# Two Strassen operands of a squared-ReLU layer: made where they are used, or made early and carried through DRAM

## The chip, the cores and the metric

The kernel runs on one core of a Trainium2 chip. The metric is the device time of one execution in microseconds (us). Runs of one set were taken on one chip, next to runs of the kernel before. Of each kernel one execution was also recorded by the hardware profiler. TensorE does the matmuls here and writes their sums into PSUM tiles; VectorE and ScalarE empty these (a "bank-emptying addition" is a VectorE operation that does so), and GpSimd does some of the elementwise work.

## The reference

```python
# attention: 8 batches, 8 heads, 576 positions, head size 64, all float32
scores = q @ k.T / sqrt(64)
ret = (scores * Dmat) @ v             # Dmat: gamma_h ** (i - j) for i >= j, else 0
x = ret as (4608 tokens, 512)
# feed-forward, d_ff 2048
h = maximum(x @ w_in, 0)
out = (h * h) @ w_out                 # g below is h * h, transposed
```

## The kernel before

The two large products are done by a Strassen-like scheme with seven products in place of eight, twice nested in the second one. A block is 512 tokens, and there are nine.

*First half.* For each block and for each of four slices of d_ff (`mp`), seven products (`j` = 0 to 6) give the four quarters of g. VectorE then makes four more operands from them, and all seven go to DRAM. The attention of later tokens runs between the products.

*Second half.* Each of the seven operands of each of the nine blocks is one round (63 rounds, `k`): it is fetched from DRAM, divided again into four, VectorE makes four inner sums, and TensorE does seven small products of eight matmuls.

```python
PRODUCTS = (("A11", "B11", "a"), ("S2", "T2", "b"), ("S1", "T1", "c"), ("A12", "B21", "a"),
            ("S3", "T3", "b"), ("S4", "B22", "c"), ("A22", "T4", "b"))   # left, right, PSUM bank

    def g_sums(n, mp):                       # first half, after product 6 of a slice
        g = g_of(mp)
        return [                             # one of them behind each of the next products
            lambda: nc.vector.tensor_tensor(g["S1"], g["S3"], g["A22"], op=ALU.add),       # L555
            lambda: nc.vector.tensor_tensor(g["S2"], g["S1"], g["A11"], op=ALU.subtract),  # L556
            lambda: nc.vector.tensor_tensor(g["S3"], g["A11"], g["S3"], op=ALU.subtract),  # L557
            lambda: nc.vector.tensor_tensor(g["S4"], g["A12"], g["S2"], op=ALU.subtract),  # L558
            lambda: nc.sync.dma_start(g_dram[n, :, :, 2 * mp:2 * mp + 2, :]..., g_room[mp % 2]...),
        ]
    # ... cut: in ffn_in, the additions that empty PSUM banks
        elif j == 1: nc.vector.tensor_tensor(u2, p, p1, op=ALU.add)                        # L629
        elif j == 2: nc.vector.tensor_tensor(p15, p, p1, op=ALU.add)                       # L631
        elif j == 4: nc.vector.tensor_tensor(g["A22"], p, p15, op=ALU.add)                 # L636
        elif j == 5: nc.vector.tensor_tensor(g["S3"], p, u2, op=ALU.add)                   # L640
        else:        nc.vector.tensor_tensor(g["A12"], p, p1, op=ALU.add)                  # L643
    # ... cut: the second half's loop
    for k in range(N_K + 1):
        sums_next = inner_sums(k + 1)        # four VectorE operations, L859 to L862
        inner(k, 0)                          # one small product: 8 matmuls, L909
        for e in range(3):
            inner(k - 1, 4 + e)              # product 4 is emptied by L925, needed by product 6
            if e == 2: outer(k - 1)          # up to two additions, L964
            inner(k, 1 + e)
            sums_next[e]()
            f = next(steps_0, None); f and f()   # block 0's own sums, in narrow strips
        sums_next[3]()
        fetch_g(k + 4)
```

The order in which each engine gets its work is the order of this code. Block 0 takes another path: it is multiplied without the seven products, stored, and its sums are made strip by strip during the second half (`sums_0`).

Of the kernel before, what the change touches and what calls it, by code (L numbers as in the profile page):

```python
# [9 lines left out]
F32 = mybir.dt.float32  # L10
# [3 lines left out]
ALU = mybir.AluOpType  # L14
# [4 lines left out]
HT = TOK // 2  # L19
# [7 lines left out]
PRODUCTS = (  # L27
    ("A11", "B11", "a"),
    ("S2", "T2", "b"),
    ("S1", "T1", "c"),  # L30
    ("A12", "B21", "a"),
    ("S3", "T3", "b"),
    ("S4", "B22", "c"),
    ("A22", "T4", "b"),
)
# [5 lines left out]
def kernel(  # L41
# [33 lines left out]
    nc = tc.nc  # L75
# [9 lines left out]
    N_M = N_DF // 2  # L85
    N_MP = N_M // 2
    N_MQ = N_M // 2
    N_BLK = n_tok // TOK
    NP = len(PRODUCTS)
# [5 lines left out]
    dram = ctx.enter_context(tc.tile_pool(name="dram", bufs=1, space=bass.MemoryType.DRAM))  # L95
# [18 lines left out]
    WI_SLOT = {n: j for j, n in enumerate(("A11", "A12", "S3", "A22", "S1", "S2", "S4"))}  # L114
    w_out = [W[(4 + j) % NP].rearrange("p (m s f) -> p m s f", m=N_MQ, s=NP) for j in range(NP)]
    WO_SLOT = {n: j for j, n in enumerate(("B11", "T3", "B21", "B22", "T1", "T2", "T4"))}
    w2_dram = dram.tile([NP, 128, N_MQ, NP * 128], F32, name="w2_dram")
    g_dram = dram.tile([N_BLK, NP, 128, N_M, HT], F32, name="g_dram")

    room = const.tile([128, 15872], F32, name="room")  # L120
    g_room = [room[:, j * 3584:(j + 1) * 3584].rearrange("p (s m t) -> p s m t", s=NP, m=2) for j in range(2)]
    p_room = [room[:, 7168 + j * 1536:7168 + (j + 1) * 1536].rearrange("p (s m t) -> p s m t", s=3, m=2) for j in range(2)]
    xs_room = room[:, 10240:11776].rearrange("p (s c t) -> p s c t", s=3, c=2)
    xT_room = [room[:, 11776 + j * 2048:11776 + (j + 1) * 2048].rearrange("p (c t) -> p c t", c=N_DM) for j in range(2)]
    G_ORDER = tuple(p[0] for p in PRODUCTS)
    QUARTERS = ((0, 1), (3, 5), (6, 7))
    SUMS = ((1, 3), (4, 6))
    assert G_ORDER == ("A11", "S2", "S1", "A12", "S3", "S4", "A22")

    loaded = {}  # L130
    N_EARLY = TOK // C
# [104 lines left out]
    def sum_w_in(mp):  # L236

        a11, a12, a21, a22, s1, s2, s4 = (w_in[mp][:, :, j, :, :].rearrange("p m c f -> p m (c f)") for j in range(NP))
        return [lambda: nc.vector.tensor_tensor(s1, a21, a22, op=ALU.add),
                lambda: nc.vector.tensor_tensor(s2, s1, a11, op=ALU.subtract),  # L240
                lambda: nc.vector.tensor_tensor(s4, a12, s2, op=ALU.subtract),
                lambda: nc.vector.tensor_tensor(a21, a11, a21, op=ALU.subtract)]
# [93 lines left out]
    for half in range(2):  # L336
        at = slice(CH * half, CH * half + CH)
# [191 lines left out]
    def fetch_w2(j):  # L529
        nc.sync.dma_start(w_out[j].rearrange("p m s f -> p m (s f)"), w2_dram[WO_SLOT[PRODUCTS[j][1]], :, :, :])  # L530

# [14 lines left out]
    sums = {}  # L546

    def g_of(mp):
        return {name: g_room[mp % 2][:, s, :, :] for s, name in enumerate(G_ORDER)}

    def g_sums(n, mp):

        g = g_of(mp)
        return [
            lambda: nc.vector.tensor_tensor(g["S1"], g["S3"], g["A22"], op=ALU.add),  # L555
            lambda: nc.vector.tensor_tensor(g["S2"], g["S1"], g["A11"], op=ALU.subtract),  # L556
            lambda: nc.vector.tensor_tensor(g["S3"], g["A11"], g["S3"], op=ALU.subtract),  # L557
            lambda: nc.vector.tensor_tensor(g["S4"], g["A12"], g["S2"], op=ALU.subtract),  # L558
            lambda: nc.sync.dma_start(g_dram[n, :, :, 2 * mp:2 * mp + 2, :].rearrange("s p m t -> p s (m t)"),
                                      g_room[mp % 2].rearrange("p s m t -> p s (m t)")),  # L560
        ]
# [4 lines left out]
    def some(count=1):  # L566
        for f in queue[:count]:
            f and f()
        del queue[:count]

    def first_in(j, halves=(0, 1)):

        assert n_made[0] > j
        wi, m, e = pieces[j]
        mp, mm = divmod(m, 2)
        p = ps_f.tile([128, 2, HT], F32, tag="f", name="h_ps")
        w = w_in[mp][:, mm, 2 * e:2 * e + 2, :, :].rearrange("p s c f -> p (s c) f")
        lo, hi = halves[0], halves[-1] + 1
        p = p[:, lo:hi, :]
        for c in range(N_DM):  # L580
            nc.tensor.matmul(p.rearrange("p h t -> p (h t)"), lhsT=w[:, c, :], rhs=xT[0][:, c, lo * HT:hi * HT],  # L581
                             start=(c == 0), stop=(c == N_DM - 1))

        t = g_room[mp % 2][:, 3:7:3, mm, :] if e else g_room[mp % 2][:, 0:5:4, mm, :]
        t = t[:, lo:hi, :]
        nc.scalar.activation(t, p, AF.Relu)

        some(2)
        queue.append(lambda: nc.vector.tensor_tensor(t, t, t, op=ALU.mult))
        if mm and e and hi == 2:  # L590
            queue.append(lambda: [nc.sync.dma_start(
                g_dram[0, a:b, :, 2 * mp:2 * mp + 2, :].rearrange("s p m t -> p s (m t)"),
                g_room[mp % 2][:, a:b, :, :].rearrange("p s m t -> p s (m t)")) for a, b in QUARTERS])
        if j >= N_W1 - 4:

            sums_w.setdefault(0, sum_w_in(0)).pop(0)()
            if n_next[0] > 1:
                if 1 not in sums_x:
                    sums_x[1] = sum_x(1)
                sums_x[1].pop(0)()  # L600
# [74 lines left out]
    def block_steps(n):  # L675
        if n == 0:
            seconds = [(0, first_in, j, (1,)) for j in range(N_HALF)]
            return seconds + [(0, first_in, j) for j in range(N_HALF, N_W1)]
        return [(n, ffn_in, n, mp, j) for mp in range(N_MP) for j in range(NP)]

    def step():
        n, f, *args = steps.pop(0)
        done[0] += 1
        f(*args)
# [141 lines left out]
    late1 = ctx.enter_context(tc.tile_pool(name="late1", bufs=1))  # L826
# [9 lines left out]
    N_K = N_BLK * NP  # L836
    BLOCKS = list(range(1, N_BLK)) + [0]

    def A(k):
        return A_room[k % len(A_room)].rearrange("p (m t) -> p m t", m=N_M)  # L840

    def fetch_g(k):
        if k < N_K:
            nc.sync.dma_start(A(k), g_dram[BLOCKS[k // NP], k % NP, :, :, :])

    def lefts(k):

# [24 lines left out]
    def sums_0():  # L872

        for m in range(N_M):
            t = late1.tile([128, NP, HT], F32, tag="g0", name="g0")

            def move(parts, out):
                for a, b in parts:
                    there = g_dram[0, a:b, :, m, :].rearrange("s p t -> p s t")
                    nc.sync.dma_start(*((there, t[:, a:b, :]) if out else (t[:, a:b, :], there)))  # L880

            a11, s2, s1, a12, s3, s4, a22 = (t[:, j, :] for j in range(NP))
            yield lambda: move(QUARTERS, False)
            for _ in range(8):
                yield None
            for to, x, y, op in ((s1, s3, a22, ALU.add), (s2, s1, a11, ALU.subtract), (s3, a11, s3, ALU.subtract),
                                 (s4, a12, s2, ALU.subtract)):
                yield lambda to=to, x=x, y=y, op=op: nc.vector.tensor_tensor(to, x, y, op=op)
            yield lambda: move(SUMS, True)
            for _ in range(3):  # L890
                yield None
# [3 lines left out]
    def inner(k, i):  # L895
# [12 lines left out]
        for m in range(N_MQ):  # L908
            nc.tensor.matmul(p, lhsT=s["lefts"][left][:, m, :], rhs=w_out[j][:, m, WO_SLOT[right], :],  # L909
                             start=(i in OPENS and m == 0), stop=(i in CLOSES and m == N_MQ - 1),  # L910
# [60 lines left out]
    n_last = 0  # L971
    while steps:
        n, f, *args = steps[0]
        if n == N_BLK - 1:
            if n_last in (0, 5, 10, 15):
                fetch_g(n_last // 5)
            if n_last in (2, 9, 16, 23):
                fetch_w2(2 + n_last // 7)
            if n_last == N_MP * NP - 5:
                for f in inner_sums(0):  # L980
                    f()
            n_last += 1
        step()
    some(len(queue))
    fetch_w2(NP - 1)
    steps_0 = sums_0()
    for k in range(N_K + 1):
        assert k + 4 < N_K - NP or next(steps_0, None) is None
        sums_next = inner_sums(k + 1)
        if k < N_K:  # L990
            inner(k, 0)
        for e in range(3):
            if k > 0:
                inner(k - 1, 4 + e)
            if e == 2 and k > 0:
                outer(k - 1)
            if k < N_K:
                inner(k, 1 + e)
            if sums_next[e]:
                sums_next[e]()  # L1000
            f = next(steps_0, None)
            f and f()
        if sums_next[3]:
            sums_next[3]()
        fetch_g(k + 4)


# [44 lines left out]
```

## Time and profile before

| | before |
|---|---|
| first set: median (range), runs | 990.98 (989.02 to 992.9), 3 |
| span of the profiled execution | 987.4 us |
| TensorE matmul / weight load / VectorE busy | 98% / 87% / 78% of the span |
| DMA traffic | 219 MB |

The views that matter are shown in the prediction. To read them: L909 is a line of the program; `h_a`, `h_b`, `h_c` are PSUM tiles of the first half and `o_a`, `o_b`, `o_c` those of the second; `x8` counts merged instructions; a bracket at the end of a line is the time for which the engine sat idle before it, and what ended that.

### The profile page before, as it was taken

The numbers are of one execution on the slowest core, as the hardware profiler recorded it, in microseconds if no ns is written. First come the engines' busy times: TensorE is split into PE (matmuls) and PEld (weight loads), VectorE is DVE, ScalarE is ACT, GpSimd is POOL, SyncE is SP. The second block draws the span as 40 slices with busy tenths as digits, with TensorE's granted clock in tenths as the row PEclk, the third lists the DMA queues.
The fourth block names the chain that finished last, engine by engine and source line by source line (L and its number), as shares of the span: only waits on it lengthen the run. The fifth ranks groups of instructions, "written<-read, shape, count | busy, mean of one in ns | idle before, by whom it ended". The sixth has DMA issues, their size and how long they took to land.

```text
span 987.4 us, 24367 instructions
## 1 busy us (share of the span) xinstructions
PE 967.8 (98%) x10404; PEld 863.0 (87%) x10404; DVE 769.7 (78%) x1434; ACT 234.1 (24%) x573; POOL 127.8 (13%) x121
## 2 busy tenths in 40 slices
PE   7899999999999999999999999999999999999998
PEld 6645787888888888888888889999999999999998
DVE  4889898768888988888886677777777777777765
ACT  3454573752223222322211100000000000000000
POOL 3221222312213121222201000000000000000000
PEclk7999999999999999999999999999999999999999
DMA  9985657755687687779449999675584657556351
GB/s 203 244 223 152 175 158 214 194 144 182 216 278 241 186 277 229 222 234 264 143 179 333 403 383 346 227 280 163 223 282 145 258 206 274 192 203 217 125 214 44
DMA packets 185037, 219.22 MB, mean 222 GB/s; under 512 B 118624, under 2 KB 135008, under 8 KB 175968
## 3 DMA queue, kind: packets, MB, share of 16 engines
q1 hardware_dynamic: 182816, 217.13, 67.3%
q8 instruction: 82, 1.34, 0.6%
q10 hardware_dynamic: 2112, 0.52, 0.3%
q14 instruction: 27, 0.22, 0.1%
HBM read 128.23 MB, written 89.39 MB: 220 GB/s over the span
## 4 chain that ended last, share of the span: by engine, by line
PE 88%; DVE 9%; issue 1%; DMA 1%; ACT 1%; SPq 0%; DVEq 0%; ACTq 0%
PE o_b L909 17%; PE h_b L617 15%; PE o_c L909 11%; PE o_a L909 11%; PE h_a L617 10%; PE h_c L617 10%; PE h_ps L581 4%; PE x_ps L458 3%; PE sc_ps L436 2%; PE x_ps L493 2%; PE t_ps L415 2%; DVE room L624 1%; DVE w L229 1%; PE u_ps L461 1%; DMA w<-in_moe_w_in_dram 1%
## 5 line engine op out<-in xcount | busy, mean ns | idle before, releaser
L617 PE MATMUL h_b<-room,w 128*128 128x256 f32 x736 | 177.4, 384 | 3.6 <-DVE room L636 2.6
L617 PEld LDWEIGHTS h_b<-room,w 128*128 128x128 f32 x736 | 137.3, 190 | 24.4 <-DVE room L636 3.8
L909 PE MATMUL o_b<-w,room 128*128 128x128 f32 x1168 | 144.5, 276 | 0.2 <-DVE room L860 0.2
L909 PEld LDWEIGHTS o_b<-w,room 128*128 128x128 f32 x1168 | 137.3, 192 | 0.5 <-DVE room L860 0.4
L909 PE MATMUL o_c<-w,room 128*128 128x128 f32 x1008 | 123.0, 275 | 0.0
L909 PEld LDWEIGHTS o_c<-w,room 128*128 128x128 f32 x1008 | 117.7, 192 | 0.0
L617 PE MATMUL h_c<-room,w 128*128 128x256 f32 x480 | 114.4, 382 | 0.7 <-DVE room L631 0.7
L617 PE MATMUL h_a<-room,w 128*128 128x256 f32 x448 | 107.5, 383 | 0.0
L617 PEld LDWEIGHTS h_c<-room,w 128*128 128x128 f32 x480 | 90.6, 190 | 13.3 <-DVE room L631 1.1
L617 PEld LDWEIGHTS h_a<-room,w 128*128 128x128 f32 x448 | 84.0, 190 | 11.6
L909 PE MATMUL o_a<-w,a 128*128 128x128 f32 x688 | 85.6, 275 | 0.0
L634 POOL TENSOR_TENSOR room<-room 128x512 f32<-128x512 f32 x32 | 35.7, 1116 | 364.4 <-ACT room L633 304.4
L909 PEld LDWEIGHTS o_a<-w,a 128*128 128x128 f32 x688 | 81.3, 192 | 0.1
L923 ACT COPY r<-o_a 128x128 f32<-128x128 f32 x53 | 14.1, 265 | 271.7 <-PE o_a L909 235.8
L624 DVE SCALAR_TENSOR_TENSOR room<-room 128x512 f32<-128x512 f32 x96 | 70.3, 733 | 3.3
L581 PE MATMUL h_ps<-room,w 128*128 128x512 f32 (+1 forms) x152 | 59.6, 540 | 1.1 <-ACT room L515 0.7
L376 POOL TENSOR_TENSOR q_ld<-q_ld,dv 128x512 f32<-128x512 f32 (+1 forms) x39 | 46.9, 1202 | 81.6 <-DMA q_ld<-in_q_dram 78.1
L636 DVE TENSOR_TENSOR room<-h_b,room 128x512 f32<-128x512 f32 x32 | 22.1, 689 | 41.9 <-PE h_b L617 40.1
L458 PEld LDWEIGHTS x_ps<-qk,v_ld 64*64 64x64 f32 x1152 | 40.2, 137 | 14.4 <-issue 11.5
L458 PE MATMUL x_ps<-qk,v_ld 64*64 64x64 f32 x1152 | 49.6, 226 | 1.9 <-ACT u_sb L496 1.9
L581 PEld LDWEIGHTS h_ps<-room,w 128*128 128x128 f32 x152 | 28.2, 194 | 24.0 <-issue 20.5
L404 ACT COPY qk<-flip 32x256 f32<-32x256 f32 x120 | 48.3, 402 | 1.7
(111 smaller groups left out, 1440.5 us busy)
## 6 DMA issues: line engine op xcount, KB each, us to landing
g_dram<-room SPq DMA_DIRECT2D x32, 1792.0 KB, 7.4
a<-g_dram SPq DMA_DIRECT2D x43, 1024.0 KB, 7.1
room<-g_dram SPq DMA_DIRECT2D x20, 1024.0 KB, 6.5
w<-w_dram SPq DMA_DIRECT2D x7, 1792.0 KB, 12.3
out_dram<-room SPq DMA_DIRECT2D x17, 512.0 KB, 3.3
w<-in_moe_w_in_dram SPq DMA_DIRECT2D x16, 512.0 KB, 6.0
w<-in_moe_w_out_dram SPq DMA_DIRECT2D x16, 512.0 KB, 4.2
v_ld<-in_v_dram SPq DMA_DIRECT2D x31, 256.0 KB, 3.6
```

Of the source, the lines that this page charges most:

```text
L376: engine.tensor_tensor(t, t, dv[:cs, :, NCH + ci:NCH + ci + 1].to_broadcast([cs, H, D]), op=ALU.mult)
L404: nc.scalar.copy(*moves.pop(0)[1:])
L415: nc.tensor.transpose(p[:, h, j, hp, :], loaded[i][j][rows(h), 2 * hp:2 * hp + 2, :], ident[rows(h), rows(h)])
L436: nc.tensor.matmul(sc[e][rows(h), hp, :], lhsT=kT[rows(e), hp, t], rhs=qT[rows(e), hp, t], start=True, stop=True, skip_group_check=True)
L458: own.append(lambda hp=hp, e=e, b=b: nc.tensor.matmul(x_at(hp, b, h), lhsT=s["vs"][rows(h), 2 * hp + b, :], rhs=s["ret"][rows(h), e, hp, : ...
L493: nc.tensor.matmul(x_at(hp, b, h), lhsT=u[rows(e), hp, :], rhs=s["qT"][rows(e), hp, CH * h:CH * h + CH], start=clears(b, hp // 2), stop=Fa ...
L581: nc.tensor.matmul(p.rearrange("p h t -> p (h t)"), lhsT=w[:, c, :], rhs=xT[0][:, c, lo * HT:hi * HT], start=(c == 0), stop=(c == N_DM - 1))
L617: nc.tensor.matmul(p[:, mm, :], lhsT=w[:, c, :], rhs=xs[n][right][:, c, :], start=(j in OPENS and mm == 0 and c == 0), stop=(j in CLOSES a ...
L624: nc.vector.scalar_tensor_tensor(t, t, 0.0, t, op0=ALU.max, op1=ALU.mult)
L634: nc.gpsimd.tensor_tensor(g["A11"], g["A11"], g["A11"], op=ALU.mult)
L636: nc.vector.tensor_tensor(g["A22"], p, p15, op=ALU.add)
L909: nc.tensor.matmul(p, lhsT=s["lefts"][left][:, m, :], rhs=w_out[j][:, m, WO_SLOT[right], :], start=(i in OPENS and m == 0), stop=(i in CLO ...
```

## The change

The intent: S2 = S1 − A11 and S4 = A12 − S2 can be made from operands that are on chip in the second half anyway. So they need not be made in the first half, nor written, nor read. Two of VectorE's four sums per slice go from the first half, whose VectorE is the busier one (84% against 74%), to the second; five operands instead of seven go through DRAM. Since S1 must be there before S2 is made, it is fetched one round earlier.

```diff
--- before.py
+++ after.py
@@ -114,18 +114,17 @@
     WI_SLOT = {n: j for j, n in enumerate(("A11", "A12", "S3", "A22", "S1", "S2", "S4"))}
     w_out = [W[(4 + j) % NP].rearrange("p (m s f) -> p m s f", m=N_MQ, s=NP) for j in range(NP)]
     WO_SLOT = {n: j for j, n in enumerate(("B11", "T3", "B21", "B22", "T1", "T2", "T4"))}
+    G_KEPT = ("A11", "S1", "A12", "S3", "A22")
     w2_dram = dram.tile([NP, 128, N_MQ, NP * 128], F32, name="w2_dram")
-    g_dram = dram.tile([N_BLK, NP, 128, N_M, HT], F32, name="g_dram")
+    g_dram = dram.tile([N_BLK, len(G_KEPT), 128, N_M, HT], F32, name="g_dram")
 
     room = const.tile([128, 15872], F32, name="room")
-    g_room = [room[:, j * 3584:(j + 1) * 3584].rearrange("p (s m t) -> p s m t", s=NP, m=2) for j in range(2)]
+    g_room = [room[:, j * 2560:(j + 1) * 2560].rearrange("p (s m t) -> p s m t", s=5, m=2) for j in range(2)]
     p_room = [room[:, 7168 + j * 1536:7168 + (j + 1) * 1536].rearrange("p (s m t) -> p s m t", s=3, m=2) for j in range(2)]
     xs_room = room[:, 10240:11776].rearrange("p (s c t) -> p s c t", s=3, c=2)
     xT_room = [room[:, 11776 + j * 2048:11776 + (j + 1) * 2048].rearrange("p (c t) -> p c t", c=N_DM) for j in range(2)]
-    G_ORDER = tuple(p[0] for p in PRODUCTS)
-    QUARTERS = ((0, 1), (3, 5), (6, 7))
-    SUMS = ((1, 3), (4, 6))
-    assert G_ORDER == ("A11", "S2", "S1", "A12", "S3", "S4", "A22")
+    QUARTERS = ((0, 1), (2, 5))
+    SUMS = ((1, 2), (3, 4))
 
     loaded = {}
     N_EARLY = TOK // C
@@ -546,16 +545,14 @@
     sums = {}
 
     def g_of(mp):
-        return {name: g_room[mp % 2][:, s, :, :] for s, name in enumerate(G_ORDER)}
+        return {name: g_room[mp % 2][:, s, :, :] for s, name in enumerate(G_KEPT)}
 
     def g_sums(n, mp):
 
         g = g_of(mp)
         return [
             lambda: nc.vector.tensor_tensor(g["S1"], g["S3"], g["A22"], op=ALU.add),
-            lambda: nc.vector.tensor_tensor(g["S2"], g["S1"], g["A11"], op=ALU.subtract),
             lambda: nc.vector.tensor_tensor(g["S3"], g["A11"], g["S3"], op=ALU.subtract),
-            lambda: nc.vector.tensor_tensor(g["S4"], g["A12"], g["S2"], op=ALU.subtract),
             lambda: nc.sync.dma_start(g_dram[n, :, :, 2 * mp:2 * mp + 2, :].rearrange("s p m t -> p s (m t)"),
                                       g_room[mp % 2].rearrange("p s m t -> p s (m t)")),
         ]
@@ -581,7 +578,7 @@
             nc.tensor.matmul(p.rearrange("p h t -> p (h t)"), lhsT=w[:, c, :], rhs=xT[0][:, c, lo * HT:hi * HT],
                              start=(c == 0), stop=(c == N_DM - 1))
 
-        t = g_room[mp % 2][:, 3:7:3, mm, :] if e else g_room[mp % 2][:, 0:5:4, mm, :]
+        t = g_room[mp % 2][:, 2:5:2, mm, :] if e else g_room[mp % 2][:, 0:4:3, mm, :]
         t = t[:, lo:hi, :]
         nc.scalar.activation(t, p, AF.Relu)
 
@@ -840,8 +837,19 @@
         return A_room[k % len(A_room)].rearrange("p (m t) -> p m t", m=N_M)
 
     def fetch_g(k):
-        if k < N_K:
-            nc.sync.dma_start(A(k), g_dram[BLOCKS[k // NP], k % NP, :, :, :])
+
+        j = k % NP
+        if k < N_K and j not in (2, 5):
+            k += j == 1
+            nc.sync.dma_start(A(k), g_dram[BLOCKS[k // NP], G_KEPT.index(PRODUCTS[k % NP][0]), :, :, :])
+
+    def made(k):
+
+        if k >= N_K or k % NP not in (1, 5):
+            return []
+        x, y = (k + 1, k - 1) if k % NP == 1 else (k - 2, k - 4)
+        at = [slice(2 * e, 2 * e + 2) for e in range(4)]
+        return [lambda at=at: nc.vector.tensor_tensor(A(k)[:, at, :], A(x)[:, at, :], A(y)[:, at, :], op=ALU.subtract) for at in at]
 
     def lefts(k):
 
@@ -872,19 +880,18 @@
     def sums_0():
 
         for m in range(N_M):
-            t = late1.tile([128, NP, HT], F32, tag="g0", name="g0")
+            t = late1.tile([128, len(G_KEPT), HT], F32, tag="g0", name="g0")
 
             def move(parts, out):
                 for a, b in parts:
                     there = g_dram[0, a:b, :, m, :].rearrange("s p t -> p s t")
                     nc.sync.dma_start(*((there, t[:, a:b, :]) if out else (t[:, a:b, :], there)))
 
-            a11, s2, s1, a12, s3, s4, a22 = (t[:, j, :] for j in range(NP))
+            a11, s1, a12, s3, a22 = (t[:, j, :] for j in range(len(G_KEPT)))
             yield lambda: move(QUARTERS, False)
-            for _ in range(8):
+            for _ in range(6):
                 yield None
-            for to, x, y, op in ((s1, s3, a22, ALU.add), (s2, s1, a11, ALU.subtract), (s3, a11, s3, ALU.subtract),
-                                 (s4, a12, s2, ALU.subtract)):
+            for to, x, y, op in ((s1, s3, a22, ALU.add), (s3, a11, s3, ALU.subtract)):
                 yield lambda to=to, x=x, y=y, op=op: nc.vector.tensor_tensor(to, x, y, op=op)
             yield lambda: move(SUMS, True)
             for _ in range(3):
@@ -979,12 +986,15 @@
             if n_last == N_MP * NP - 5:
                 for f in inner_sums(0):
                     f()
+            if n_last >= N_MP * NP - 4:
+                made(1)[n_last - N_MP * NP]()
             n_last += 1
         step()
     some(len(queue))
     fetch_w2(NP - 1)
     steps_0 = sums_0()
     for k in range(N_K + 1):
+        sums_g = [None] * (k % NP == NP - 1) + made(k + 2)
         assert k + 4 < N_K - NP or next(steps_0, None) is None
         sums_next = inner_sums(k + 1)
         if k < N_K:
@@ -998,10 +1008,15 @@
                 inner(k, 1 + e)
             if sums_next[e]:
                 sums_next[e]()
-            f = next(steps_0, None)
+            if sums_g:
+                f = sums_g.pop(0)
+            else:
+                f = next(steps_0, None)
             f and f()
         if sums_next[3]:
             sums_next[3]()
+        for f in sums_g:
+            f()
         fetch_g(k + 4)
 
 
```

## The prediction

> **What bounds the kernel now.** I first read the page's busy times, then the stretch table for three stages: attention interleaved with the first half of the feed-forward (to 545 us), the last first-half block (to 589), and the second half.
>
> ```profile
> core 0: us, PE busy (x) PEld busy (x) DVE busy (x) ACT busy (x) POOL busy (x), PEclk, DMA share, GB/s
> 108.00:545.00 437.00, 430.45 (x5174) 365.87 (x5173) 365.59 (x588) 149.34 (x343) 95.62 (x84) 1.00 0.70 218
> 545.00:589.00 44.00, 44.00 (x206) 38.82 (x205) 31.72 (x48) 4.14 (x7) 4.15 (x4) 1.00 0.99 396
> 589.00:981.00 392.00, 391.76 (x3504) 391.40 (x3503) 289.44 (x664) 33.16 (x125) 0.00 (x0) 1.00 0.60 215
> ```
>
> The columns are busy us with instruction counts, then granted clock, DMA share and GB/s. TensorE has no room in the last stage: 391.76 of 392 us. In the first it is idle 437 − 430.45 = 6.55 us. VectorE is busy 84% of the first stage and 74% of the last, so it has room in both. DMA is nearly full only from 545 to 589, and TensorE loses nothing there (44.00 of 44).
>
> Next I read TensorE's waits in the first stage (two windows, 110 to 300 and 300 to 545): line, what it waited for, total us, times, longest.
>
> ```profile
> PE h_b L617 <- DVE room L636: 2.0, 2, 1.7
> PE h_b L617 <- DVE room L542: 1.0, 1, 1.0
> PE h_c L617 <- DVE room L631: 0.7, 1, 0.7
> ...
> PE x_ps L458 <- ACT u_sb L496: 1.4, 2, 1.0
> PE sc_ps L436 <- DVE qk L419: 0.7, 1, 0.7
> PE h_b L617 <- DVE room L636: 0.6, 1, 0.6
> ```
>
> They sum to 6.4 us, 5.0 of it behind VectorE. This is the whole prize of the first stage: whatever VectorE is spared, TensorE cannot gain more. The timeline of VectorE around the worst one shows the mechanism:
>
> ```profile
> 147.49 1.50 POOL L376 TENSOR_TENSOR q_ld<-q_ld,dv 128x512 f32<-128x512 f32 x1
> ...
> 148.60 0.94 DVE L558 TENSOR_TENSOR room<-room 128x512 f32<-128x512 f32 x1
> 149.47 1.54 DVE L240 TENSOR_TENSOR w<-w 128x512 f32<-128x512 f32 x1
> 151.04 0.69 DVE L241 TENSOR_TENSOR w<-w 128x512 f32<-128x512 f32 x1
> 151.65 0.68 DVE L636 TENSOR_TENSOR room<-h_b,room 128x512 f32<-128x512 f32 x1
> ...
> 152.38 0.92 PE L617 MATMUL h_b<-room,w 128*128 128x256 f32 x3 [1.66 <-DVE room L636]
> ```
>
> L636, which empties the PSUM bank TensorE needs next, stands behind L558 (S4 of g), a removed operation.
>
> Last, VectorE's timeline of one second-half round, for how far it may run behind:
>
> ```profile
> 701.81 0.29 DVE L925 TENSOR_TENSOR r<-o_b,small 128x128 f32<-128x128 f32 x1 [0.46 <-PE o_b L909]
> 702.78 0.29 DVE L919 TENSOR_TENSOR small<-o_b,small 128x128 f32<-128x128 f32 x1 [0.67 <-PE o_b L909]
> ...
> 704.49 0.29 DVE L921 TENSOR_TENSOR small<-o_c,small 128x128 f32<-128x128 f32 x1 [0.60 <-PE o_c L909]
> ...
> 706.32 0.68 DVE L861 TENSOR_TENSOR room<-a 128x512 f32<-128x512 f32 x1
> 706.92 0.68 DVE L862 TENSOR_TENSOR room<-a,room 128x512 f32<-128x512 f32 x1
> 708.07 0.29 DVE L925 TENSOR_TENSOR r<-o_b,small 128x128 f32<-128x128 f32 x1 [0.46 <-PE o_b L909]
> ```
>
> L925 recurs after 6.26 us: one round, seven groups of eight matmuls, 0.893 us a group. Operations listed at 0.68 us start 0.60 us apart, so 0.605 us is the price of one 128x512 addition in a full queue. VectorE's spare time per round is the sum of the brackets: 0.46 + 0.67 + 0.60 = 1.73 us.
>
> **What the Trainium skill says.** "Perfetto Trace Analysis", section "Identifying the Most-Contended Engine", calls matmul busy share a poor measure and recommends the weight-load share. Here that is 391.40/392 in the second half and 365.87/437 = 84% in the first; the 98% of the first stage hides short gaps, but the trace names no releaser for most of them. "TensorE: Matmul & The Clock Gate", section "Architectural detail", says VectorE's queue is strict FIFO; the wait of L636 behind L240 and L241 agrees, and it means that each added quarter delays every bank-emptying addition behind it. "SBUF — State Buffer", section "SBUF: two separate sides", says a VectorE operation with two SBUF inputs and a GpSimd operation exclude one another for a whole instruction; L240's 1.54 us beside GpSimd against 0.68 agrees. In the second half GpSimd runs nothing, so the moved operations cost 0.605 us there and sometimes twice that where they are removed.
>
> **The change part by part.**
> *Removed, first half:* L556 and L558, 32 each at 708 and 709 ns in the group view; in a full queue about 64 x 0.605 = 38.7 us of VectorE. Little of it lies on the path. I went through the stalls one by one. At 147 and 150 us (0.65 + 1.66) L557 and L558 stood in front; S3 now comes one product earlier, so some 1.5 us disappear from the queue and I count 1.7 with the slowdown beside GpSimd. At 134 us (0.31 shown, some 0.45 in start times) L558 was in front: −0.4. At 430 us (0.59 shown, some 0.75) all three of L556 to L558: −0.7. At 489 us TensorE waited 0.98 for ScalarE's L496, which stood behind a conversion waiting for VectorE's L211, behind L556 and L557: −1.0. At 292 us (0.95) and 322 us (0.73) none of the removed ones is close ahead: −0.4 for both. Sum: −4.2 us.
>
> *Removed, traffic:* two of seven operands are neither written nor read: 2 x 9 blocks x 2 directions x 1.05 MB = 38 MB of 219. No TensorE wait for DMA is listed in these stretches: 0 us.
>
> *Added, second half:* per block of seven rounds, two operands of four quarters: 8 x 0.605 = 4.84 us, 11% of the 43.8 us of a block. They sit in two rounds only. In the round that makes S4, one quarter fits into the 0.60 gap; three follow: 3 x 0.605 − 0.46 = 1.35 us late at the next L925. In the round that makes S2 the first slot is empty, so all four come after the second inner sum: 4 x 0.605 − 0.46 = 1.96 us late. Deadline: TensorE's seventh product adds into the bank that L925 reads. It starts 5 groups (4.47 us) into the round; L925 normally ends 2.27 us into it. So 2.2 us of lateness are free. Both rounds pass, the second with 0.2 us left; the next round's 1.73 us bring VectorE back. I put +0.5 us for nine blocks, for an occasional miss. The first block's strip sums lose two of four operations, but they filled gaps: 0.
>
> *Moved, transition:* four quarters of the first S2 are placed between the last four products of the first half. VectorE was only just in time there: L643 starts at 589.35 after a 0.22 us wait, and the first-half bank it empties is the one that the second matmul group of the second half takes, at 590.04. Four quarters put 4 x 0.605 = 2.4 us ahead of it, minus L558 (1.35 us there, beside GpSimd) and the 0.22: L643 ends about 0.9 us or, with a GpSimd collision, 1.5 us late. TensorE waits +1.2 us. The wait for L860 at 595 us (some 0.4) is then covered, since S2 and S4 no longer stand in front: −0.4. Sum +0.8.
>
> *Total:* −4.2 + 0.5 + 0.8 = −2.9 us: 991.0 − 2.9, rounded to 988.
>
> **The rivals.**
> (a) *VectorE becomes the bound of the second half.* If all added work were exposed, 9 x 4.84 = 44 us: 1035. Against it: after the change VectorE is busy some (289 + 9 x 8 x 0.684)/392 = 86%. A milder form is likelier: each S2 round misses its deadline by 0.5 us, 9 x 0.5 = 4.5 us, giving 992. The 0.2 us margin is its argument.
> (b) *VectorE is the hidden pacer of the first half.* Then much of 38.7 us comes back: 955 to 970. For it: 84% busy and many short gaps. Against: only 6.4 us of named waits, and the stages without waits on VectorE run at the same matmul spacing.
> (c) *DMA was binding from 545 to 589.* At 0.99 share, 17% less traffic looks like several us. But TensorE was busy 44.00 of 44: no change from it.
> (d) *Everything first-half is recovered and the rest is free:* 991 − 6.4 = 984.6.
>
> **Range and chances.** The ends follow from (d), lower by some 2 us for unnamed gaps, and from the mild (a) with no first-half relief: 982.5 to 992.5. The before runs alone spread from 989.0 to 992.9. A gain over 2% (20 us) needs (b): 0.03. A loss over 2% needs (a) in earnest: 0.02.
>
> **What would show each step.** Right: second-half TensorE busy still within 1 us of the stretch; VectorE 86% there; waits on VectorE lines in the first half 2 to 3 us instead of 5.0; a new wait of about 1 us on L643's counterpart at the transition; bytes down from 219 to about 181 MB. Wrong: in the second half, waits of matmuls of product seven on the addition of product five that recur in each block (mild a); a first stage shorter by more than 7 us (b); a stretch before the transition that shortens without fewer VectorE waits (c).

## The result, and the profile after

| | before | changed |
|---|---|---|
| median of the runs (range) | 990.86 (989.02 to 992.9), 4 | 985.65 (985.29 to 986.0), 4 |
| span of the profiled execution | 987.4 | 983.9 |
| VectorE busy, share of the span | 78% | 77% |
| traffic | 219.22 MB | 181.46 MB |

The ratio is 0.9947, 95% interval 0.9927 to 0.9967. (Ratios are the mean time of one kernel's fast runs over that of the other's of the same rounds, so not quite the ratio of the medians quoted.) It is a real gain, of half a per cent, and by a 2% measure "same".

The lines have moved: of the bank-emptying additions L629, L631, L636, L640, L643 are now L626, L628, L633, L637, L640 (so L640 is now the one of product 6, before it was that of product 5); L909 is L916, L925 is L932, L859 to L862 are L867 to L870; the weight sums L239 to L242 are L238 to L241. L852 is new: it makes a quarter of S2 or S4.

The same three stretches, with the columns as in the prediction:

```profile
108.00:545.00 437.00, 434.11 (x5196) 369.48 (x5195) 332.80 (x536) 149.75 (x344) 92.94 (x85) 1.00 0.61 190
545.00:589.00 44.00, 44.00 (x222) 39.09 (x220) 30.91 (x46) 3.81 (x7) 4.13 (x4) 1.00 0.82 307
589.00:981.00 392.00, 391.23 (x3497) 390.46 (x3495) 317.28 (x714) 32.88 (x124) 0.00 (x0) 1.00 0.45 161
```

VectorE lost 365.59 − 332.80 = 32.8 us in the first stretch, and TensorE is busy 3.7 us more of it (the stretches are fixed in time, so this one holds a little more of the changed kernel's work). In the last one VectorE went from 289 to 317 us, 81%, and TensorE lost 0.5 us.

TensorE's waits from 110 to 545 us:

```profile
PE h_b L614 <- DVE room L541: 1.0, 1, 1.0
PE x_ps L457 <- ACT u_sb L495: 0.8, 2, 0.4
PE sc_ps L435 <- DVE qk L418: 0.7, 1, 0.7
PE h_b L614 <- DVE room L633: 0.2, 1, 0.2
```

Of 6.4 us, 2.7 are left, 1.9 of them behind VectorE (5.0 before; the prediction said 2 to 3). The list is short of the true loss: at 134 us it has 0.31 us before the change, while TensorE's start times below lose 0.63 there. The listed waits fell by 3.7 us, the start times gained 4.6. The waits for L631 and most of those for L636 are gone, and ScalarE's L496 (now L495) costs 0.8 instead of 1.4.

The place of the worst stall, at 150 us. In the kernel before, these two stood, among others, ahead of the lines that the prediction shows:

```profile
145.96 0.67 DVE L557 TENSOR_TENSOR room<-room 128x512 f32<-128x512 f32 x1
146.55 1.52 DVE L239 TENSOR_TENSOR w<-w 128x512 f32<-128x512 f32 x1
```

In the changed kernel, GpSimd first, then VectorE and TensorE:

```profile
148.73 1.50 POOL L445 TENSOR_TENSOR v_ld<-v_ld,dv 128x512 f32<-128x512 f32 x1
...
145.60 0.67 DVE L238 TENSOR_TENSOR w<-w 128x512 f32<-128x512 f32 x1
...
146.79 1.06 DVE L239 TENSOR_TENSOR w<-w 128x512 f32<-128x512 f32 x1
147.89 1.43 DVE L240 TENSOR_TENSOR w<-w 128x512 f32<-128x512 f32 x1
149.24 0.68 DVE L633 TENSOR_TENSOR room<-h_b,room 128x512 f32<-128x512 f32 x1
...
149.97 1.99 PE L614 MATMUL h_b<-room,w 128*128 128x256 f32 x8 [0.19 <-DVE room L633]
```

S3's and S4's additions (L557, L558) no longer stand between the weight sums. The weight sums L238, L239 and L240 here are L239, L240 and L241 of the kernel before. L633 starts at 149.24 instead of 151.65, and TensorE waits 0.19 us instead of 1.66.

A round of the second half in which S2 is made, VectorE's timeline first, then TensorE's:

```profile
670.05 0.68 DVE L868 TENSOR_TENSOR room<-room,a 128x512 f32<-128x512 f32 x1
670.65 0.69 DVE L852 TENSOR_TENSOR a<-room,a 128x512 f32<-128x512 f32 x1
...
672.78 0.69 DVE L852 TENSOR_TENSOR a<-room,a 128x512 f32<-128x512 f32 x1
673.38 0.69 DVE L870 TENSOR_TENSOR room<-a,room 128x512 f32<-128x512 f32 x1
673.99 1.29 DVE L852 TENSOR_TENSOR a<-room,a 128x512 f32<-128x512 f32 x2
675.19 0.29 DVE L932 TENSOR_TENSOR r<-o_b,small 128x128 f32<-128x128 f32 x1
...
675.90 1.06 PE L916 MATMUL o_b<-w,a 128*128 128x128 f32 x8
```

The four quarters stand one behind the second inner sum, one behind the third and two behind the fourth. L932 has no bracket any more: VectorE came to it late. It ends at 675.48, and the product that needs it starts at 675.90, without a bracket: 0.42 us were to spare.

*Where the time went.* TensorE executes the same 10,404 matmuls in both programs, so its instructions can be paired by number, and the difference of their start times shows where one trace falls behind the other. In the next table the first trace of the changed kernel is the zero, and differences are counted from its time 120 us, so that the start-up of the kernel is left out. A column says how many us a trace is behind when the changed kernel's is at that time.

| trace, us behind at | 140 | 148.5 | 152 | 300 | 440 | 500 | 586 | 600 | 620 | 980 |
|---|---|---|---|---|---|---|---|---|---|---|
| before | 0.63 | 1.67 | 3.14 | 3.13 | 3.98 | 4.57 | 4.56 | 4.69 | 4.11 | 4.11 |
| before, second trace | 0.64 | 1.68 | 3.14 | 3.13 | 4.01 | 4.60 | 4.59 | 4.72 | 3.96 | 3.96 |
| changed, second trace | 0.00 | 0.00 | 0.00 | -0.02 | -0.01 | 0.00 | 0.00 | 0.00 | 0.24 | 0.24 |
| changed, third trace | 0.00 | 0.00 | 0.00 | -0.02 | -0.01 | -0.01 | -0.02 | -0.03 | -0.07 | -0.06 |

The gain is five steps in the first half, 4.57 us together: 0.63 at 134 us, 1.04 at 148, 1.47 at 150, 0.85 at 430 and 0.59 at 489. Between them the programs run at the same pace to 0.02 us. The transition to the second half gains another 0.13, and the first block of the second half gives 0.58 back. From 620 us on, eight blocks with the added work cost nothing.

*The start-up* is what scatters. The 1,390th TensorE instruction starts at 100.5 us in both traces of before, and at 101.2, 102.9 and 100.2 us in the three of the changed kernel. So one pair of traces alone, 987.4 against 983.9, understates the gain by 0.7 us; the medians of three sets show 4.7 to 5.2 us (990.86 to 985.65, 990.47 to 985.78, 990.18 to 985.43), of which the traces name 4.1. Where the other 0.6 to 1.1 us come from is not shown: the traced start-ups of the changed kernel are not the earlier ones on the whole.

### The profile page after: what moved, and what is told of

The parts are those of the page before. It is cut to its first block, busy times and chain, and to the rows that moved or that the text cites. A ratio compares the mean times of both kernels' runs of the same rounds, so it can differ in the third digit from the quotient of the medians.

```text
span 983.9 us, 24277 instructions
## 1 busy us (share of the span) xinstructions
PE 968.0 (98%) x10404; PEld 863.3 (88%) x10404; DVE 759.3 (77%) x1426; ACT 233.9 (24%) x573; POOL 124.8 (13%) x121
## 2 busy tenths in 40 slices
DMA packets 172012, 181.46 MB, mean 184 GB/s; under 512 B 118144, under 2 KB 132480, under 8 KB 165248
## 4 chain that ended last, share of the span: by engine, by line
PE 87%; DVE 8%; DMA 2%; ACT 1%; issue 1%; SPq 0%; DVEq 0%; ACTq 0%
PE o_b L916 16%; PE h_b L614 15%; PE o_a L916 11%; PE o_c L916 11%; PE h_a L614 10%; PE h_c L614 10%; PE h_ps L578 4%; PE x_ps L457 3%; PE x_ps L492 2%; PE sc_ps L435 2%; PE t_ps L414 2%; DMA g<-g_dram 1%; DVE room L621 1%; DVE w L222 1%; DVE w L225 1%
## 5 line engine op out<-in xcount | busy, mean ns | idle before, releaser
L916 PE MATMUL o_b<-w,room 128*128 128x128 f32 x1168 | 144.4, 275 | 0.2 <-DVE room L868 0.2
L916 PEld LDWEIGHTS o_b<-w,room 128*128 128x128 f32 x1168 | 137.2, 192 | 0.4 <-DVE room L868 0.4
L916 PE MATMUL o_c<-w,room 128*128 128x128 f32 x1008 | 123.0, 275 | 0.0
L916 PEld LDWEIGHTS o_c<-w,room 128*128 128x128 f32 x1008 | 117.7, 192 | 0.0
L916 PE MATMUL o_a<-w,a 128*128 128x128 f32 x688 | 85.6, 275 | 0.0
L916 PEld LDWEIGHTS o_a<-w,a 128*128 128x128 f32 x688 | 81.2, 192 | 0.1
L631 POOL TENSOR_TENSOR room<-room 128x512 f32<-128x512 f32 x32 | 34.0, 1062 | 366.4 <-ACT room L630 295.6
L633 DVE TENSOR_TENSOR room<-h_b,room 128x512 f32<-128x512 f32 x32 | 22.1, 690 | 51.0 <-PE h_b L614 47.5
## 6 DMA issues: line engine op xcount, KB each, us to landing
w<-w_dram SPq DMA_DIRECT2D x7, 1792.0 KB, 10.8
```

What stands on the lines that cost most here:

```text
L631: nc.gpsimd.tensor_tensor(g["A11"], g["A11"], g["A11"], op=ALU.mult)
L916: nc.tensor.matmul(p, lhsT=s["lefts"][left][:, m, :], rhs=w_out[j][:, m, WO_SLOT[right], :], start=(i in OPENS and m == 0), stop=(i in CLO ...
```

## The experiments

The theory, Q: what TensorE gained is the shorter queue of VectorE in front of the bank-emptying additions, stall by stall; the traffic gave nothing; the second half stays free of cost because each added operation ends before a deadline that can be worked out. The main rival, D: the gain is the 38 MB of traffic. Twelve runs were made, of eight new kernels and of the two given ones; all gave correct results, and four sets were timed or looked at together. The table behind each is the same as above.

**The kernel before, again.** No edit.

> The kernel before, run again for the spread of its own stalls. Theory Q (the gain is the queue of VectorE in front of the bank-emptying additions): the same five stalls of TensorE in the first half as in its first profile (near 134, 148, 150, 430 and 489 us, some 4.5 us in start times together), ratio to itself 1.000, runs within 989 to 993. Rival D (the gain is the 38 MB of traffic): says nothing of this run. If the stalls differ by over 1 us from the first profile, the spread of its times (989.0 to 992.9) is in them.

Measured: 989.62 us median (989.06 to 990.55), ratio 1.0003 (0.9987 to 1.0020). Its row is the second of the table above: the same five stalls to within 0.04 us. The spread of the kernel's times is not in them.

**S2 and S4 put back into VectorE's queue, traffic as changed.**

```diff
+    idle_room = [room[:, 6144 + j * 512:6656 + j * 512].rearrange(...) for j in range(2)]   # read by nobody
             lambda: ... g["S1"], g["S3"], g["A22"], op=ALU.add),
+            lambda: nc.vector.tensor_tensor(idle_room[0], g["S1"], g["A11"], op=ALU.subtract),
             lambda: ... g["S3"], g["A11"], g["S3"], op=ALU.subtract),
+            lambda: nc.vector.tensor_tensor(idle_room[1], g["A12"], idle_room[0], op=ALU.subtract),
```

> The changed kernel, with the two removed additions put back into VectorE's queue of the first half at their old places, writing into a spare room that nobody reads; the traffic stays at five operands. Theory Q: the first-half stalls come back, +4 to +5 us, about 990. Rival D: no change, 985.7 within 1.

| us behind the changed kernel at | 140 | 148.5 | 152 | 300 | 440 | 500 | 586 | 600 | 620 | 980 |
|---|---|---|---|---|---|---|---|---|---|---|
| S2 and S4 back in the queue | 0.65 | 1.69 | 3.16 | 3.14 | 4.01 | 4.60 | 5.61 | 6.82 | 6.06 | 6.06 |

Measured: 991.21 us (990.89 to 992.02), ratio to before 1.0017 (1.0003 to 1.0032). TensorE's waits from 110 to 545 us are again those of the kernel before, line by line:

```profile
PE h_b L617 <- DVE room L636: 2.6, 3, 1.7
PE x_ps L458 <- ACT u_sb L496: 1.4, 2, 1.0
...
PE h_c L617 <- DVE room L631: 0.7, 1, 0.7
```

All five steps came back at their places with their sizes, with the smaller traffic. D is refuted as the cause of the first half's gain. The run also shows a cost that was not expected: 2.2 us at the transition, where the put-back sums and the four quarters of the first S2 meet. The change pays nothing there only because it takes S2 and S4 away at the same place.

**S4 alone put back, S2's place left empty.**

```diff
             lambda: ... g["S1"], g["S3"], g["A22"], op=ALU.add),
+            None,
             lambda: ... g["S3"], g["A11"], g["S3"], op=ALU.subtract),
+            lambda: nc.vector.tensor_tensor(idle_room[1], g["A12"], g["A11"], op=ALU.subtract),
```

> As the last, but only S4's addition is put back, at its old place, S2's place is left empty. Theory Q, stall by stall: S4's addition stood in front at 134 (+0.5), 148 to 150 (+0.9 to +1.5) and 430 (+0 to +0.7), not at 489 (0): +1.5 to +2.7 us in all, about 987.7, and no stall over 0.7 us at the 489 us place. Rival D: 985.7 within 1. A third reading, that any addition costs its 0.6 us wherever it stands, would give 32 x 0.6 = 19 us, about 1005.

| us behind the changed kernel at | 140 | 148.5 | 152 | 300 | 440 | 500 | 586 | 600 | 620 | 980 |
|---|---|---|---|---|---|---|---|---|---|---|
| S4 back in the queue | 0.00 | 0.00 | 1.48 | 1.46 | 1.48 | 1.49 | 2.50 | 3.11 | 2.65 | 2.65 |

Measured: 987.28 us (987.10 to 987.84), ratio 0.9977. The sum was met, in part by luck: the first half gave 1.49, the lowest that was expected, and the rest came from a place that was not named. At 150 us it cost 1.48, and at 489 nothing, as expected; but at 134 and 430 us it cost nothing either, and 1.6 us came at the transition. So stalls do not add up operation by operation: one operation ahead was absorbed at 134 and 430, two were not. The third reading, 0.6 us for each of the 32 additions wherever they stand, would have given 1005 and is far off.

**The traffic put back, VectorE's work as changed.**

```diff
# ... cut: g_dram has room for seven operands again
-            lambda: nc.sync.dma_start(g_dram[n, :, ...], g_room[mp % 2]...),
+            lambda: [nc.sync.dma_start(g_dram[n, a:a + b, ...], g_room[mp % 2][:, 0:b]...) for a, b in ((0, 5), (5, 2))],
...
+        if k < N_K and j in (0, 5) and BLOCKS[k // NP]:
+            nc.sync.dma_start(A(k + (j == 0)), g_dram[BLOCKS[k // NP], 5 + (j == 5), :, :, :])
```

> The changed kernel with the traffic put back: in the eight blocks of the first half two more operands are written, copies of A11 and S1, and in the second half they are fetched into the tiles of S2 and S4 before those are made; VectorE's work stays as changed. 33.6 MB more, about 215 MB. Theory Q: 985.7 within 1. Rival D: +4 to +5 us, about 990.

| us behind the changed kernel at | 140 | 148.5 | 152 | 300 | 440 | 500 | 586 | 600 | 620 | 980 |
|---|---|---|---|---|---|---|---|---|---|---|
| traffic back, 215 MB | 0.00 | 0.00 | 0.00 | -0.02 | -0.01 | 0.00 | -0.01 | -0.01 | 3.59 | 3.59 |

Measured: 988.33 us (986.83 to 988.74), ratio 0.9984 (0.9970 to 0.9999): outside what Q expected, and near D's size, yet at another place than D's. In the whole first half the traffic makes no difference of more than 0.02 us. All of the loss is one event at 606 us. VectorE's waits from 590 to 630 us in this run:

```profile
DVE g L897 <- DMA g<-g_dram: 4.7, 1, 4.7
...
DVE room L854 <- DMA room<-g_dram: 1.2, 1, 1.2
```

and in the changed kernel:

```profile
DVE g L895 <- DMA g<-g_dram: 2.4, 1, 2.4
```

The first strip of block 0 lands late, VectorE stands still for it with everything behind it in its queue, and TensorE then waits 2.6 us for an addition. In the changed kernel VectorE's wait for the same strip is half as long. The second wait, 1.2 us, is an artefact of this experiment: it is for a fetch into the tile of S4, which the changed kernel does not have. So the traffic is no source of the first half's gain; at the one crowded place it can cost. How much of the 3.6 us is the delayed strip alone was not separated.

**The changed kernel, again**, as yardstick of the next three.

> The changed kernel again, as the yardstick of this set: 985.3 to 986.0, the same stalls of TensorE as in its first profile (0.57 us near 149, 1.18 near 289, 0.61 near 486, 0.50 near 591, 0.49 near 606 and 0.29 near 613, in start times), ratio 0.993 to 0.997.

Measured: 985.78 us (984.75 to 987.47), ratio 0.9945 (0.9921 to 0.9968). The four times lie wider apart than the 985.3 to 986.0 that was expected. Its trace is a row of the first table: equal to the first trace within 0.02 us from 120 to 600 us.

**Two more quarters in each S2 round.**

```diff
         sums_g = [None] * (k % NP == NP - 1) + made(k + 2)
+        if k % NP == NP - 1:
+            sums_g += made(k + 2)[2:]
```

> The changed kernel with the last two quarters of S2 made twice, at the end of the same round (same values). The changed kernel leaves L932's addition 1.81 us late after an S2 round, with 0.42 us of slack before TensorE's seventh product. Theory Q with the deadline of the prediction: lateness 1.81 + 2 x 0.605 = 3.02, so the product waits 3.02 - 2.23 = 0.79 us in each of the eight S2 rounds inside the second half, and nowhere else: +6.3 us, about 992. Rival H (in the second half VectorE's order does not matter below full occupancy; 16 additions raise it from 81% to 83%): no change, 985.7. Rival S (each addition simply adds its 0.6 us): +9.7 us, about 995.

Measured: 992.59 us (992.20 to 994.27), 6.8 us over the changed kernel of this set. From 620 to 980 us its trace falls 7.51 us behind (from −0.24 to 7.27), in eight equal steps of 0.94, one per S2 round. TensorE's waits from 600 us on:

```profile
PE o_b L916 <- DVE r L932: 5.4, 8, 0.7
```

Eight waits (5.4 us as listed, 7.5 in start times) at the place and on the addition that the deadline names. The size expected was 0.79 each, so the model is 0.15 us short; rival H (free, 985.7) and rival S (9.7 us) are out. This is the limit of the change: VectorE is far from full, 81% before the extra operations, and two operations of 0.6 us at the wrong place of one round in seven cost more than the change has won.

**Strips of block 0 later.**

```diff
-            for _ in range(6):
+            for _ in range(6 + 3 * (m == 0)):
                 yield None
```

> The changed kernel with three more empty steps between the load of the first strip of block 0 and its first addition. Theory L (the 2.39 us in which VectorE waited for that strip made the two stalls near 606 and 613): both go, -0.8 us, about 984.9, and VectorE's wait for g's DMA is under 0.3 us. Rival M (the added quarters of the first block make them, by being packed closer than in later blocks): both stay, 985.7.

Measured: 985.05 us (984.68 to 985.18), ratio 0.9940. In the trace both stalls, near 606 and 613 us, are gone: −0.77 us at 620, and VectorE no longer waits for the strip. Theory L holds, M falls: the quarters of the first block are not at fault. The change itself had brought the strip's first addition forward: its diff cuts the empty steps between a strip's load and this addition from eight to six. VectorE was ready for it 10.8 us after the load was issued (590.42 to 601.19), in the kernel before 17.7 us after (594.46 to 612.17, 2.5 of them a wait for another load). By the times alone (0.7 us in medians) one would not say so; the trace decides.

**Four more operations ahead of the sixth product's addition, and ahead of the seventh's**.

```diff
             if n_last >= N_MP * NP - 4:
                 made(1)[n_last - N_MP * NP]()
+            if n_last == N_MP * NP - 2:        # second kernel: - 1
+                for f in made(1):
+                    f()
```

> The changed kernel with the four quarters of the first S2 made a second time (same values), just ahead of the addition that empties the bank of the sixth product (L637) of the last first-half step: that addition ends 4 x 0.605 = 2.4 us later. Theory B6 (the second matmul group of the second half takes the bank of the sixth product): the group, which in the changed kernel started at once, now waits about 1.6 us (586.2 to 587.8). Theory B7 (as the prediction took it, the bank of the seventh product): the changed kernel's trace already speaks against it, since the group started before L640; here it would wait until L640 has ended, some 3.5 us. In both the span grows by about 2.4 us in all, the rest of it at the first S2 of the inner sums (591 us).

> As the last, but the second making stands behind the sixth product's addition (L637) and ahead of the seventh's (L640). Theory B6: the second group starts without a wait, the whole 2.4 us are seen at the first S2 of the inner sums (591 us). Theory B7: the second group waits about 3.5 us.

First the changed kernel's own lines at the transition, TensorE's and then VectorE's:

```profile
586.21 1.06 PE L916 MATMUL o_b<-w,room 128*128 128x128 f32 x8
...
584.67 0.68 DVE L637 TENSOR_TENSOR room<-h_c,room 128x512 f32<-128x512 f32 x1
...
586.59 0.69 DVE L640 TENSOR_TENSOR room<-h_b,room 128x512 f32<-128x512 f32 x1
```

The second group of the second half starts at 586.21, before the seventh product's bank has been touched (L640, 586.59), so it cannot be waiting for that. With the operations ahead of the sixth, TensorE's waits from 545 us on begin with:

```profile
PE o_b L916 <- DVE room L637: 1.4, 1, 1.4
```

The group now waits, for the sixth product's addition. With the operations behind that addition it does not wait at all; the loss, 2.4 us in both, then comes 3.6 us later, behind L926 and not at the inner sum as expected. Theory B6 holds: the bank that the group takes is the sixth product's. The single times, 987.71 and 988.60 us, agree roughly with the 2.6 and 2.8 us by which the traces end behind; the changed kernel was not run in that set.

**VectorE's order at three places**, an attempt to beat both kernels.

```diff
-        if mp == N_MP - 1 and j in (3, 4, 5) and n_next[0] > n + 1:       # a sum of x for the next block,
+        if mp == N_MP - 1 and j in (3, 4, 5, 6) and n_next[0] > n + 1:    # ahead of S1 of g
...
-    some(len(queue))                 # the last S3 of g and its store
-    fetch_w2(NP - 1)                 # the last weights
...
             f and f()
+            if k == 0 and e == 1:    # now behind the second inner sum of the first round
+                some(len(queue))
+                fetch_w2(NP - 1)
```

> An attempt to beat both kernels by VectorE's order alone: the last S3 of g, its store and the last weight load go behind the second inner sum of the first round of the second half (so the strip load goes ahead of two large transfers), and the second sum of x for the next block goes ahead of S1 of g. Theory Q: the stalls near 289 (-1.0), 591 (-0.5) and 606 to 613 (-0.8) go: -2.3 us, about 983.4. If only the transfers were moved by it and the queue does not matter: -0.8, about 984.9.

Measured: 984.50 us, but with four times between 982.55 and 988.38, ratio 0.9940 (0.9910 to 0.9970) against the changed kernel's 0.9945: inconclusive. So it was run again with more rounds, beside the changed kernel.

> The reordered kernel again, since its four times lay between 982.6 and 988.4 although its trace lost the stalls it was meant to lose. Theory Q with start-up noise: its trace from 50 us on is 2.2 to 2.5 us shorter than the changed kernel's of the same set, whatever the times; the median of six times is 1 to 3 us lower than the changed kernel's. If the order cost something that the one profile did not show: stalls of over 0.5 us at new places after 50 us.

> The changed kernel as the yardstick of this pair: 985 to 987, the stalls after 50 us as in its two earlier traces (near 149, 289, 486, 591, 606 and 613 us); differences between its own runs lie in the first 50 us.

Measured: 982.45 us (981.80 to 983.87, 6 runs), against 985.43 (984.47 to 989.45, 6 runs) of the changed kernel and 990.18 (988.98 to 993.57, 11 runs) of before. Ratios to before: 0.9922 (0.9908 to 0.9935) and 0.9960 (0.9941 to 0.9979), which do not overlap. The changed kernel's trace in this set is the last row of the first table: equal to its first within 0.07 us.

| us behind the changed kernel at | 152 | 300 | 440 | 500 | 586 | 600 | 620 | 980 |
|---|---|---|---|---|---|---|---|---|
| reordered, first trace | -0.41 | -1.43 | -1.42 | -1.41 | -1.41 | -1.90 | -2.66 | -2.66 |
| reordered, repeat | 0.00 | -1.00 | -0.99 | -0.99 | -0.99 | -1.48 | -2.24 | -2.24 |

The three steps are 1.0 at 289, 0.5 at 591 and 0.8 at 606 to 613 us, as expected. The first trace had won 0.46 more near 148 us, which the repeat does not show. Which of the three moves gave the steps at 591 and at 606 to 613 us was not separated (the strips placed later had given the last one alone). What TensorE waits for in the repeat, from 110 us to the end, is

```profile
PE x_ps L457 <- ACT u_sb L495: 0.8, 2, 0.4
PE sc_ps L435 <- DVE qk L418: 0.7, 1, 0.7
PE h_b L614 <- DVE room L633: 0.2, 1, 0.2
```

This version beats both kernels: by the medians it is 7.7 us under the kernel before, by the traces from 120 us on about 6.3 us. In the five traces named above the first 100 us differ by up to 2.7 us, and no experiment here touched those.

## Why the prediction was right or wrong

The range (982.5 to 992.5) held the 985.65, and "within 2%" was right. The direction and the mechanism were right, the size was too small: −2.9 us forecast, −4.1 in the traces from 120 us on, −5.2 in the medians of the first set. By its steps:

| step | forecast | traces |
|---|---|---|
| stall at 134 us | −0.4 | −0.63 |
| stalls at 147 and 150 us | −1.7 | −2.51 |
| stall at 430 us | −0.7 | −0.85 |
| stall at 489 us | −1.0 | −0.59 |
| stalls at 292 and 322 us | −0.4 | 0.0 |
| traffic | 0 | 0 in the first half (tested); not separated at 606 us |
| second half | +0.5 | +0.58, in its first block alone |
| transition | +0.8 | −0.13 |

**First half: right, the largest term mis-sized.** The prediction named the five places, and the experiment with the sums put back returned each. For the pair at 147 and 150 us it counted 1.5 us of removed queue time and 0.2 for the slowdown beside GpSimd; the pair gave 1.04 + 1.47 = 2.51. Redone from the two traces: from the first operation behind L629 to the start of L636 VectorE took 5.69 us before (145.96 to 151.65), and takes 3.64 now (145.60 to 149.24, L238 to L633), 2.05 less. L557 and L558 made up 0.59 + 0.87 = 1.46 of that, from start to start, as counted. The other 0.59 is the slowdown, counted as 0.2: the three weight sums beside GpSimd's operations took 1.52 + 1.54 + 0.69 = 3.75 us before and take 0.67 + 1.06 + 1.43 = 3.16 now. The last 0.46 was left out: against TensorE's matmuls, L629 itself had already started 0.46 us later before the change, in a queue of VectorE that shows no idle time since the stall at 134 us. At 489 us the prediction took both L556 and L557 as gone from the front; but S3 moved into S2's place, so that one addition of 0.60 us went, and 0.59 was won. At 292 and 322 us nothing removed stood close ahead and nothing was won, as argued; the 0.4 put down for chance was wrong. That the sum of the first half came so near (−4.2 against −4.58) is in part luck: one term was short by 0.8 and two were over by 0.4 each. The reordering experiment shows that the first of these is a queue stall all the same: it went when another operation was moved.

**Transition: wrong, and this is the step that failed.** It read: "the first-half bank it empties is the one that the second matmul group of the second half takes, at 590.04". That rested on a coincidence of times, L643's end and the group's start, and on a guess about which of three banks is handed out next. The group takes the bank of the sixth product. That addition ended at 585.35 (584.67 + 0.68), 0.86 us before the group's turn, so no stall arose. The stretch is not free in general: with S2 and S4 put back TensorE lost 2.2 us in it, at other waits, and four more operations lost it 2.4. The second part of the term, −0.4 for the wait on L860, was not won either: the last S1 and S3 and the quarters fill the queue as S1 to S4 had done before, and the wait near 591 us is still there (0.50 us from one matmul's start to the next, 0.51 before, of which the inner sum's L868 is the named cause). It went only by reordering. Replacing +0.8 by −0.1 brings the sum to −3.8.

**Second half: the deadline was right, the reason for the cost wrong, its size right by luck.** Forecast was that L925's addition would be late by 1.35 us in S4 rounds and 1.96 in S2 rounds, with 2.2 allowed. In the trace (start of the addition against the end of the product that it empties) it is 1.21 and 1.81 late, round after round, with 1.02 and 0.42 us left before TensorE's product 6. The deadline itself was tested by the two extra quarters. The +0.5 was set aside for occasional misses of it; there are none outside the first block, and there the cause is a strip for which VectorE, now ready earlier, waits 2.4 us, which the prediction had put down as costing nothing ("they filled gaps: 0"). Its strict-FIFO argument, from the Trainium skill ("TensorE: Matmul & The Clock Gate", section "Architectural detail"), covers this case too: VectorE's 2.39 us wait for a DMA held up everything behind it.

**Busy share of VectorE: 81%, not 86%.** The forecast multiplied 72 operations by the listed 0.684 us, left out the 16 strip operations that go, and the four quarters that are made before the second half. Operations back to back also start 0.60 us apart, so their listed times overlap.

**The rivals.** (a), VectorE as the bound of the second half, did not happen, but the experiment shows that it was 0.42 us away. (b), a hidden pacer worth up to 38.7 us, is out: between its stalls the first half runs at the same pace to 0.02 us whether VectorE has the sums or not. (c) was rightly set aside for the stretch from 545 to 589 us: with the traffic back nothing moved there. (d), 984.6, lies nearer to the measured 985.65 than the 988 that was forecast, but not by its mechanism: it has 6.4 us won in the first half and nothing lost later, and the traces have 4.6 won and 0.6 lost.

## What to carry to other kernels

When the bound engine is 98% busy, the list of what it waits for, and not the work taken off another engine, shows the size of the relief: 32.8 us less work on VectorE gave 4.6 us, all at five named places. The list is no exact ceiling, since a listed 0.31 us was worth 0.63 here. A busy share does not tell whether work can be added to an in-order engine; find the operation that the bound engine needs next, its deadline and how late the new work makes it, and test the deadline with a little more. Pair the instructions of the bound engine in two traces and plot the difference: it shows where a few microseconds went even when run-to-run scatter hides them in the times.

## What the Trainium skill lacked or had wrong

- "TensorE: Matmul & The Clock Gate", section "Architectural detail": its strict FIFO of VectorE agrees with the traces here, and one costly form of it is not spelled out: an operation waiting 2.4 us for a DMA held back an addition for TensorE (0.77 us lost), 4.7 us in another run.
- "SBUF — State Buffer", section "SBUF: two separate sides": the exclusion of GpSimd and VectorE operations with two SBUF inputs agrees (1.43 and 1.54 us instead of 0.68). The table of waits shows only the victim, TensorE; no page says that such a lengthened operation must be looked for in VectorE's timeline.
- "Perfetto Trace Analysis", section "Identifying the Most-Contended Engine": the weight-load share showed the second half as full (390.46 of 392 us), in agreement; in the first half it read 85% (369.48 of 437 us), yet the listed waits behind VectorE were only 1.9 us there and the later reordering won 1.0, so what it suggests as room is mostly not waiting for VectorE.
- No page gives a measured start-to-start time of two VectorE additions of 128x512 float32, nor says which of its cost formulas is meant for it: 0.60 us in these traces, with 0.68 listed.
- No page has the scatter of the start-up: 100.2 to 102.9 us to the same TensorE instruction in five traces of two kernels.
